# Attention and a gated MLP in one kernel: the first q and k loads uncast over hardware queues, cast on chip, with new instruction orders

## The chip, the cores and the metric

The kernel runs on one core of a Trainium2 chip. The metric is device time in microseconds (us). A run of a kernel is one execution, and the time before is the median of three such runs. The profile is one further execution, recorded instruction by instruction.

The engines are called by their short names: PE (TensorE, the matrix engine), ACT (ScalarE), DVE (VectorE), POOL (GpSimd) and SP (SyncE, which only issues transfers here). In the trace `PEld` is the load of a matrix operand, and `SPq`, `ACTq` and `POOLq` are issues of transfers from an engine's queue.

## The reference

Eight batches of eight heads, 576 tokens, head size 64, with 16 extra "beacon" keys and values ahead of each head's own. Causal attention, then an MLP with a sigmoid gate.

```python
B, H, S, Nb, D = (8, 8, 576, 16, 64)
k_all = concatenate([beacon_k, k], axis=2); v_all = concatenate([beacon_v, v], axis=2)
scores = matmul(q, k_all.transpose(0, 1, 3, 2)) / sqrt(D)
scores = where(causal, -1e9, scores)        # beacons are never masked
a = softmax(scores)
x = matmul(a, v_all)                        # -> (B * S, H * D) = (4608, 512)
h = x @ w_in                                # 512 -> 2048
g = h * (1 / (1 + exp(-1.702 * h)))
out = g @ w_out                             # 2048 -> 512, float32
```

All inputs and the output are float32 in HBM. On chip the matrix operands are 16 bit.

## The kernel before

**Attention.** Four heads make a *set*; a batch has two sets (`HS = 2`) and there are 16 in all. A set's q and k lie in `qn` and `kn` as 128 partitions (4 heads by 32) of token rows, are turned by DVE (`e_turn`, L422 and L429) into `qT` and `kT`, and give scores in the PSUM tile `s` (`e_qk`, L458). There is one such tile, four banks large, so the scores of a chunk can only start when ACT's exp (`e_exp`, L469) has read the chunk before. The exps go to `E`; masks are applied there by DVE or POOL (`e_mask`, L483 and L490). The value products (`e_av`, L546) take v from `vb`; the same function with ones gives the sums of the softmax, which DVE turns and inverts (`e_z1` L558, `e_z2` L565 and L569) and multiplies in (`e_norm`, L581) on the way to `xT`.

**The first two sets** are worked in halves. `ENDS = ((0, S), (0, HF), (HF, S))` with `HF = 256` names the whole set and its first and second part. `load_qk(s, which, part=1)` loads the first 256 tokens and `part=2` the other 320, so that chunks `qk0` and `qk1` (the first halves of sets 0 and 1) need only the first parts; `qk2` to `qk4` are the rest of set 0 and `qk5` to `qk7` the rest of set 1.

**MLP.** Tokens are taken in groups. `m1` products (`e_m1`) of groups 0 and 1 (256 tokens each) are gated by ACT's tanh (L628) and DVE (L647), later groups (512 tokens) by ACT's gelu (L635). The second product of groups 2 to 9 is made from seven products of quarter matrices (`products`), with sums by DVE in `sA` and `tB` (L679), and joins by DVE into `osb` (L744); the first two groups use `e_m2`. All of these go through `mm`: it issues one full-width matmul (L598) or, inside short pieces of work that lie between column-tiled value products, four of 32 columns (L601). Results are stored from SP (L676, L751).

**Loads.** q, k, v and both weight matrices are loaded by POOL (`nc.gpsimd.dma_start` at L368, L376 to L387, L393, L400), which casts float32 to 16 bit during the transfer. The beacon keys (`bkf`, L406) are loaded uncast by SP and ACT and cast by DVE (L412). `pool_load` keeps eight POOL transfers in flight: a ninth depends on the end of the one eight before.

**The order.** The function lists every piece of work as an `op` of a `Plan`, with an engine, a duration, and what it depends on. Tables written out by hand or by a search beforehand (`ORDER`) give the order of the ops on each engine. `Plan.run` walks these orders with the durations, gives each op a start, and sorts all ops by start; the instructions are then emitted in that sequence. The durations decide how the engines' emissions interleave and which PSUM tile a product gets, and the order on each engine is that of the table. One exception matters here: an op is emitted on whatever engine its function calls, at the place that its op has in the sequence.

**Fill.** Ahead of `qk0` and `qk1`, PE gets float32 matmuls on a scratch area whose results nobody reads (`FILL`, L1137). The scratch lies in `sA[0]`.

```python
FILL = {"qk0": (512, 384), "qk1": (256,)}
```

Of the kernel before, what the change touches and what calls it, by code (L numbers as in the profile page):

```python
# [8 lines left out]
F32 = mybir.dt.float32  # L9
# [8 lines left out]
        80, 106, 114, 123, 126, 144, 147, 116, 119, 159, 156, 135, 165, 128, 137, 162, 140, 168, 171, 231, 131, 133,  # L18
        149, 152, 154, 236, 174, 201, 238, 177, 192, 241, 195, 198, 204, 260, 180, 186, 207, 265, 187, 181, 188,
        267, 216, 210, 189, 270, 182, 213, 217, 401, 218, 183, 219, 404, 245, 250, 248, 279, 253, 407, 274, 255,  # L20
        284, 277, 282, 414, 222, 223, 224, 312, 292, 310, 225, 296, 308, 302, 290, 306, 320, 298, 294, 300, 314,
        304, 318, 316, 435, 426, 343, 365, 344, 423, 338, 339, 340, 341, 438, 345, 346, 349, 350, 429, 464, 351,
        433, 431, 366, 574, 359, 360, 352, 354, 355, 577, 361, 356, 474, 362, 357, 477, 583, 372, 373, 367, 368,
        480, 605, 482, 374, 484, 375, 607, 510, 490, 500, 496, 610, 492, 508, 506, 504, 498, 502, 488, 494, 486,
        514, 512, 596, 516, 534, 539, 540, 535, 593, 536, 545, 541, 537, 555, 742, 546, 601, 542, 556, 547, 745,
        622, 603, 557, 548, 619, 561, 748, 599, 550, 551, 562, 563, 755, 552, 564, 553, 629, 558, 776, 568, 627,
        625, 569, 570, 779, 635, 571, 651, 647, 655, 643, 631, 649, 633, 767, 805, 764, 653, 641, 774, 637, 639,
        657, 645, 818, 661, 659, 770, 679, 815, 684, 685, 772, 680, 686, 915, 681, 821, 690, 682, 687, 825, 918,
        706, 691, 823, 692, 713, 924, 693, 714, 700, 707, 715, 946, 708, 701, 695, 696, 697, 948, 702, 716, 698,
        703, 709, 951, 833, 851, 839, 827, 1083, 853, 831, 835, 855, 829, 934, 857, 937, 841, 837, 843, 849, 960,  # L30
        847, 845, 963, 875, 876, 940, 944, 877, 880, 881, 882, 886, 1086, 942, 878, 887, 883, 888, 1089, 891, 889,
        968, 892, 902, 1096, 893, 966, 903, 970, 904, 1117, 905, 894, 896, 909, 910, 1120, 897, 911, 898, 899, 912,
        1146, 984, 996, 988, 1256, 990, 1105, 992, 994, 998, 1002, 1000, 1108, 982, 972, 974, 1159, 976, 980, 1156,
        978, 986, 1111, 1041, 1020, 1042, 1113, 1043, 1115, 1021, 1022, 1259, 1031, 1023, 1025, 1026, 1032, 1027,
        1033, 1265, 1034, 1028, 1047, 1044, 1048, 1287, 1036, 1037, 1162, 1038, 1039, 1049, 1289, 1054, 1278, 1055,
        1050, 1056, 1275, 1057, 1292, 1166, 1180, 1164, 1178, 1172, 1182, 1186, 1198, 1304, 1188, 1281, 1301, 1285,
        1170, 1192, 1194, 1174, 1190, 1283, 1184, 1168, 1307, 1176, 1221, 1196, 1222, 1216, 1311, 1217, 1223, 1224,
        1309, 1218, 1227, 1219, 1228, 1229, 1230, 1243, 1244, 1245, 1232, 1237, 1233, 1234, 1317, 1238, 1235, 1239,
        1246, 1250, 1240, 1319, 1251, 1252, 1315, 1327, 1313, 1253, 1339, 1331, 1323, 1329, 1321, 1343, 1361, 1377,
        1341, 1362, 1337, 1325, 1335, 1333, 1363, 1366, 1367, 1364, 1368, 1372, 1369, 1373, 1374, 1375, 1382, 1383,  # L40
        1388, 1378, 1384, 1379, 1389, 1395, 1396, 1397, 1380, 1385, 1390, 1391, 1419, 1429, 1401, 1398, 1411, 1407,
        1423, 1403, 1421, 1405, 1409, 1431, 1425, 1413, 1417, 1415, 1449, 1450, 1460, 1427, 1451, 1454, 1455, 1470,
        1471, 1452, 1456, 1461, 1472, 1457, 1473, 1465, 1462, 1466, 1463, 1467, 1468, 1476, 1477, 1483, 1478, 1479,
        1484, 1485, 1486,
    ],
    "ACT": [
        3, 1, 83, 85, 109, 111, 115, 117, 120, 157, 136, 160, 138, 163, 166, 141, 169, 232, 172, 237, 175, 239, 178,
        193, 242, 196, 199, 202, 261, 205, 266, 208, 268, 190, 271, 211, 214, 402, 184, 220, 405, 408, 417, 415,
        313, 293, 226, 309, 311, 297, 307, 291, 321, 303, 295, 315, 301, 305, 299, 319, 317, 436, 342, 439, 468,
        465, 575, 578, 584, 587, 606, 608, 511, 501, 491, 493, 509, 497, 499, 505, 507, 495, 489, 503, 487, 513,  # L50
        515, 517, 611, 538, 743, 746, 749, 758, 756, 777, 780, 636, 652, 648, 656, 632, 644, 650, 634, 806, 642,
        638, 654, 658, 646, 640, 662, 660, 809, 916, 683, 919, 928, 925, 947, 949, 952, 834, 840, 854, 828, 852,
        832, 836, 856, 842, 858, 830, 844, 850, 838, 848, 846, 1084, 1087, 879, 1090, 1097, 1099, 1118, 1121, 1150,
        1147, 997, 989, 991, 985, 995, 993, 1003, 983, 999, 1001, 975, 973, 977, 979, 981, 987, 1257, 1260, 1024,
        1266, 1269, 1288, 1290, 1293, 1181, 1179, 1183, 1173, 1199, 1187, 1189, 1171, 1195, 1175, 1193, 1185, 1169,
        1191, 1177, 1197, 1220, 1318, 1320, 1328, 1314, 1316, 1332, 1324, 1340, 1322, 1344, 1330, 1342, 1338, 1326,
        1336, 1334, 1365, 1420, 1430, 1408, 1412, 1404, 1422, 1424, 1402, 1406, 1426, 1410, 1414, 1432, 1416, 1418,
        1428, 1453,
    ],
    "DVE": [  # L60
        77, 103, 78, 79, 104, 105, 88, 81, 86, 82, 87, 84, 113, 110, 112, 124, 125, 145, 98, 146, 127, 148, 93, 108,
        107, 158, 228, 129, 229, 257, 130, 161, 230, 164, 167, 170, 132, 134, 150, 151, 155, 153, 259, 173, 398,
        258, 176, 179, 194, 197, 200, 203, 209, 206, 399, 400, 215, 212, 411, 412, 413, 246, 247, 251, 252, 280,
        249, 254, 256, 275, 276, 281, 283, 278, 285, 286, 419, 420, 287, 463, 288, 289, 421, 461, 580, 330, 331,
        332, 422, 462, 322, 333, 323, 326, 327, 427, 324, 428, 334, 335, 424, 328, 336, 325, 337, 329, 425, 347,
        470, 430, 434, 581, 432, 471, 353, 472, 473, 582, 475, 478, 476, 479, 358, 363, 481, 369, 739, 483, 485,
        376, 752, 370, 741, 589, 740, 590, 754, 591, 615, 592, 526, 527, 753, 597, 598, 518, 519, 522, 523, 594,
        524, 520, 525, 595, 616, 530, 617, 618, 543, 602, 521, 531, 623, 604, 549, 620, 532, 528, 621, 529, 600,
        533, 624, 804, 554, 630, 559, 760, 626, 628, 565, 802, 566, 761, 572, 803, 921, 762, 811, 763, 812, 768,
        769, 765, 766, 775, 922, 813, 814, 663, 671, 672, 673, 819, 667, 674, 668, 771, 816, 664, 820, 665, 773,  # L70
        817, 666, 669, 822, 923, 1093, 675, 1080, 688, 676, 826, 670, 677, 824, 694, 678, 1081, 930, 699, 704, 710,
        717, 711, 1082, 931, 932, 956, 957, 1095, 933, 935, 938, 936, 958, 959, 939, 859, 1094, 961, 860, 964, 871,
        867, 863, 945, 872, 861, 868, 941, 864, 865, 866, 965, 873, 943, 869, 862, 1143, 962, 884, 870, 890, 874,
        1101, 969, 1102, 971, 967, 1144, 895, 1103, 1145, 906, 900, 913, 907, 1262, 1152, 1104, 1263, 1153, 1106,
        1154, 1109, 1110, 1107, 1155, 1157, 1160, 1012, 1016, 1013, 1014, 1112, 1004, 1008, 1017, 1005, 1009, 1114,
        1015, 1264, 1116, 1010, 1161, 1018, 1006, 1011, 1271, 1158, 1029, 1007, 1272, 1035, 1019, 1273, 1274, 1040,
        1163, 1045, 1279, 1051, 1276, 1058, 1052, 1297, 1167, 1298, 1299, 1280, 1300, 1165, 1277, 1305, 1282, 1302,
        1306, 1286, 1284, 1303, 1208, 1200, 1201, 1204, 1209, 1205, 1312, 1212, 1213, 1308, 1202, 1214, 1203, 1210,
        1211, 1310, 1215, 1206, 1225, 1207, 1231, 1236, 1241, 1247, 1248, 1254, 1345, 1346, 1347, 1348, 1357, 1349,
        1350, 1351, 1358, 1353, 1354, 1359, 1360, 1352, 1355, 1370, 1356, 1376, 1381, 1386, 1392, 1393, 1399, 1433,  # L80
        1434, 1435, 1436, 1437, 1438, 1439, 1441, 1440, 1442, 1445, 1446, 1447, 1448, 1443, 1458, 1444, 1464, 1469,
        1474, 1480, 1481, 1487,
    ],
    "POOL": [
# [22 lines left out]
}  # L107


class Op:  # L110
    __slots__ = (
        "eng", "dur", "deps", "pr", "due", "emit", "kind", "ring", "mode", "lat",
        "start", "end", "left", "users", "ready", "seq", "name", "count", "table",
    )


class Plan:


# [92 lines left out]
def kernel(  # L212
# [20 lines left out]
    Q = 4  # L233
# [935 lines left out]
```

## Time and profile before

| | before |
|---|---|
| time, median of 3 runs | 338.59 us (337.24 to 339.23) |
| profiled execution: time, span | 338.63 us, 336.9 us |
| PE busy | 313.6 us, 93% of the span |
| ACT, DVE, POOL busy | 200.8, 237.2, 119.6 us |
| moved by DMA queues | 29.09 MB, of them 18.50 MB by POOL's casting loads |
| score chunk `qk0` starts | 10.88 us |
| score chunk `qk2` starts | 18.29 us |
| first `m1` product starts | 24.10 us |

The span is what the trace covers; the time also has what lies around it, 1.7 us. In the page's second part the span is cut into 40 equal slices (8.4 us each), and each digit is the busy share of one slice in tenths. Busy times of different engines overlap. `PEclk` is the granted clock of PE. A line of the chain of waits has a start, a length, and the engine and line, or the transfer, that was being waited for. A line of the list of transfers has the issuing queue, the count, the size as written on chip, and the median time from issue to landing.

### The profile page before, as it was taken

How to read it: one execution, taken by the hardware profiler on the slowest of the kernel's cores; microseconds unless marked ns; L12 is line 12 of the kernel's file. 1: busy time of each engine (PE TensorE's matmuls, PEld its weight loads, DVE VectorE, ACT ScalarE, POOL GpSimd, SP SyncE). 2: the span in 40 equal slices, each digit the busy share in tenths (PEclk: the TensorE clock that was granted, in tenths of full speed). 3: DMA queues.
4: the chain of work that ended last, by engine and by line, in shares of the span. 5: the costliest groups of instructions: out<-in, count | busy, mean ns of one | idle time of the engine just before them, and what ended most of it. 6: DMA issues, size and time to landing. Idle time of an engine off the chain costs nothing.

```text
span 336.9 us, 13766 instructions
## 1 busy us (share of the span) xinstructions
PE 313.6 (93%) x6274; PEld 221.4 (66%) x6274; DVE 237.2 (70%) x479; ACT 200.8 (60%) x236; POOL 119.6 (36%) x182
## 2 busy tenths in 40 slices
PE   3369999999989998999999899999999999999995
PEld 1256775654768466845888888657875786586484
DVE  2485944879988879997977879866986464163164
ACT  1347787765957786679767576768665503622620
POOL 7847458394131806182048204540611000000000
PEclk9998999999999999999999999999999999999999
DMA  4999999799251974696149603650230001002003
GB/s 47 171 168 181 205 172 161 153 97 189 20 101 38 159 48 66 121 133 95 28 60 157 108 6 71 110 43 5 21 101 30 4 33 62 33 31 90 6 22 105
DMA packets 61819, 29.09 MB, mean 86 GB/s; under 512 B 44352, under 2 KB 57664, under 8 KB 61760
## 3 DMA queue, kind: packets, MB, share of 16 engines
q0 software_dynamic: 51200, 18.50, 48.9%
q1 hardware_dynamic: 10464, 9.69, 8.7%
q8 instruction: 49, 0.80, 1.0%
q14 instruction: 10, 0.08, 0.1%
q10 hardware_dynamic: 96, 0.02, 0.0%
HBM read 37.22 MB, written 9.44 MB: 139 GB/s over the span
## 4 chain that ended last, share of the span: by engine, by line
PE 78%; DVE 8%; DMA 6%; ACT 4%; issue 3%; POOL 0%; DVEq 0%; ACTq 0%; POOLq 0%
PE u L598 40%; PE u L601 22%; PE u L546 8%; PE s L458 8%; DMA kn<-in_k_dram 4%; ACT E L469 3%; DMA qn<-in_q_dram 2%; DVE sA L679 1%; DVE osb L744 1%; ACT g L635 1%; DVE zs L508 1%; DVE zt L558 1%; ACT L635 1%; DVE kT L429 1%; DVE rz L569 1%
## 5 line engine op out<-in xcount | busy, mean ns | idle before, releaser
L469 ACT ACTIVATE E<-s 128x2048 f16<-128x2048 f32 (+4 forms) x66 | 98.9, 1515 | 55.6 <-PE s L458 54.1
L635 ACT ACTIVATE g<-u 128x512 f16<-128x512 f32 x128 | 69.7, 598 | 55.0 <-PE u L598 38.4
L490 POOL TENSOR_SCALAR_AFFINE_SELECT E<-E 128x512 f16<-128x512 f16 (+3 forms) x78 | 52.2, 686 | 106.4 <-ACT E L469 104.8
L598 PE MATMUL u<-xT,w 128*128 128x512 f16 (+1 forms) x456 | 87.2, 346 | 0.0
L598 PEld LDWEIGHTS <-w 128*128 128x128 f16 x456 | 44.1, 99 | 35.1 <-DVE osb L744 0.2
L744 DVE SCALAR_TENSOR_TENSOR osb<-u,osb 128x512 f32<-128x512 f32 x56 | 37.4, 683 | 24.2 <-PE u L598 21.1
L601 PE MATMUL u<-xT,w 128*32 128x512 f16 (+1 forms) x992 | 47.0, 338 | 1.1 <-issue 0.9
L458 PE MATMUL s<-qT,kT 32*128 32x32 f16 (+17 forms) x1376 | 35.6, 233 | 13.3 <-DVE kT L422 5.9
L458 PEld LDWEIGHTS <-kT 32*128 32x128 f16 x1376 | 26.0, 95 | 31.0 <-issue 19.4
L598 PE MATMUL u<-w,g 128*128 128x256 f16 (+1 forms) x232 | 37.9, 302 | 0.0
L598 PEld LDWEIGHTS <-g 128*128 128x128 f16 x324 | 30.9, 98 | 10.3
L601 PEld LDWEIGHTS <-w 128*32 128x32 f16 x992 | 27.1, 96 | 14.1 <-issue 1.9
L546 PE MATMUL u<-E,vb 128*32 128x352 f16 (+9 forms) x928 | 31.1, 266 | 1.0 <-DVE osb L744 0.4
L387 POOL DMA_DIRECT2D vb<-in_v_dram x32 | 27.5, 859 | 11.7 <-PE u L546 11.1
L581 DVE TENSOR_TENSOR xT<-u,rz 128x352 f16<-128x352 f32 (+3 forms) x48 | 25.5, 546 | 7.2 <-PE u L546 6.9
L601 PE MATMUL u<-w,g 128*32 128x256 f16 x864 | 29.7, 273 | 0.0
L546 PEld LDWEIGHTS <-vb 128*32 128x32 f16 (+1 forms) x928 | 23.7, 98 | 6.4 <-issue 1.7
L508 DVE TENSOR_TENSOR zs<-zs,E 128x1344 f16<-128x1344 f16 (+2 forms) x36 | 23.5, 654 | 5.1 <-POOL E L490 4.4
L679 DVE TENSOR_TENSOR sA<-g 128x512 f16<-128x512 f16 x32 | 13.2, 426 | 19.7 <-ACT g L635 19.6
L601 PEld LDWEIGHTS <-g 128*32 128x32 f16 x1008 | 25.9, 97 | 1.7 <-issue 0.3
L429 DVE STREAM_TRANSPOSE kT<-kn 128x576 f32<-128x576 f32 (+2 forms) x18 | 20.4, 1131 | 9.0 <-DMA kn<-in_k_dram 8.5
L598 PEld LDWEIGHTS <-sA 128*128 128x128 f16 x224 | 21.5, 98 | 3.5
(52 smaller groups left out, 335.1 us busy)
## 6 DMA issues: line engine op xcount, KB each, us to landing
out_dram<-osb SPq DMA_DIRECT2D x36, 256.0 KB, 2.8
kn<-in_k_dram POOLq DMA_DIRECT2D x14, 288.0 KB, 5.7
qn<-in_q_dram POOLq DMA_DIRECT2D x14, 288.0 KB, 5.6
vb<-in_v_dram POOLq DMA_DIRECT2D x24, 128.0 KB, 4.3
w<-in_moe_w_in_dram POOLq DMA_DIRECT2D x8, 256.0 KB, 8.4
w<-in_moe_w_out_dram POOLq DMA_DIRECT2D x4, 512.0 KB, 10.0
vb<-in_v_dram POOLq DMA_DIRECT2D x8, 112.0 KB, 5.1
vb<-in_v_dram POOLq DMA_DIRECT2D x8, 80.0 KB, 4.5
```

Source lines behind the costliest of these rows:

```text
L387: nc.gpsimd.dma_start(out=t[0 : hi - lo, j, h0:h1, :], in_=v[b, h0:h1, lo:hi, :].rearrange("h n d -> n h d"),)
L429: nc.vector.transpose(out=f32(dst.rearrange("p n e -> p (n e)")).rearrange("p (r t) -> p t r", t=n), in_=f32(src[:, a // 32 * D : e // 32 ...
L458: nc.tensor.matmul(sc[:, h, o : o + w], kT[s % NB2][r : r + 32, j * P : (j + 1) * P, d], qT[s % NB2][r : r + 32, a : a + w, d], start=(d = ...
L469: nc.scalar.activation(out=Es[s][:, :, c0:c1], in_=ss[i][:, :, o : o + c1 - c0], func=AFT.Exp, scale=0.125,)
L490: nc.gpsimd.affine_select(out=blk, in_=blk, compare_op=ALU.is_ge, fill=0.0, base=off + (Nb if j == 0 else 0), pattern=[[0, Q], [1, w]], ch ...
L508: nc.vector.tensor_tensor(out=t, in0=E[:, :, Z0:S] if i == 1 else t, in1=E[:, :, wcol[i] : wcol[i] + S - a], op=ALU.add,)
L546: nc.tensor.matmul(u[32 * h : 32 * h + 32, a:e], lhs, src[0:kw, h, col : col + e - a], start=first, stop=last,)
L581: nc.vector.tensor_tensor(out=xT[:, 2 * hs + x : 2 * hs + x + n, t0 : t0 + w], in0=rings[("av", s, x, half)][:, 0 : n * w].rearrange("p (n ...
L598: nc.tensor.matmul(o, lhs, rhs, start=start, stop=stop)
L601: nc.tensor.matmul(o[r : r + 32], lhs[:, r : r + 32], rhs, start=start, stop=stop)
L635: nc.scalar.activation(out=gts[g][:, n0:n1, 0:w], in_=rings[("m1", g, n0)][:, 0 : n * w].rearrange("p (n w) -> p n w", n=n), func=AFT.Gelu ...
L744: nc.vector.scalar_tensor_tensor(out=osbs[(g, dst)][:, :], in0=rings[("p", g, p)][:, :], scalar=scale_of(g), in1=osbs[(g, src)][:, :], op0 ...
```

## The change

**First halves and second halves of the first two sets.** The eight loads by POOL with a cast go. Instead `e_fetch` copies float32 into staging areas (`staged`) that lie in the tiles `sA` and `tB`, which nothing else uses so early, and `e_cast` casts from there into `qn` and `kn`: ACT casts the four first parts (512 columns), POOL the four second parts (640 columns).

```diff
+    def staged(s, which, part):
+        i = 2 * s + which
+        n = (ENDS[part][1] - ENDS[part][0]) // 32 * D
+        t = (sA[1], sA[2], sA[1], sA[2])[i] if part == 1 else (tB[0], tB[1], tB[2], sA[0])[i]
+        x = 4 * (i // 2) if part == 1 else 0
+        return t[:, x : x + n // (HM // 2), :].rearrange("p a n -> p (a n)").bitcast(F32)
+
+    def e_fetch(s, which, part, e):
+        b, hs = divmod(s, HS)
+        a, z = ENDS[part]
+        (nc.sync if e == "SP" else nc.scalar).dma_start(
+            out=staged(s, which, part),
+            in_=(q, k)[which][b, Q * hs : Q * hs + Q, a:z].rearrange("h (r t) d -> h r (t d)", r=32),
+        )
+
+    def e_cast(s, which, part, e):
+        a, z = ENDS[part]
+        dst = (qn, kn)[which][s % NB3][:, a // 32 * D : z // 32 * D]
+        (nc.scalar.copy if e == "ACT" else nc.gpsimd.tensor_copy)(out=dst, in_=staged(s, which, part))
...
+    def fetch_qk(s, which, part, e):
+        a, z = ENDS[part]
+        x = op(e, 450, [], lambda: e_fetch(s, which, part, e), name=f"hk{s}.{part}")
+        x = op("Q", 1560 * (z - a) / S, [x], lambda: None, name=f"hk{s}.{part}q")
+        e = ("", "ACT", "POOL")[part]
+        ld_qk[(s, which, part > 1)] = op(
+            e, 65 + 0.8345 * 2 * (z - a) if e == "ACT" else 140 + 0.95 * 2 * (z - a), [x],
+            lambda: e_cast(s, which, part, e), name=f"cast{s}.{part}",
+        )
...
-    load_bk(0, HS, (), ("SP", "ACT"))
     for s in range(HS):
-        load_qk(s, 1, part=1)
-        load_qk(s, 0, part=1)
+        fetch_qk(s, 1, 1, "SP")
+        fetch_qk(s, 0, 1, "ACT")
+        if s == 0:
+            load_bk(0, HS, (), ("SP", "ACT"))
...
     for s in range(HS):
-        load_qk(s, 1, part=2)
-        load_qk(s, 0, part=2)
+        for which in (1, 0):
+            fetch_qk(s, which, 2, "SP")
```

**Which queue they are on.** In `fetch_qk` the name `e` is given a new value before the first lambda is called. In the plan and in `ORDER` six of the eight loads are ops of SP and two of ACT. In the program that is built all eight are on ACT's queue, in this order:

```
ACT: load q0 first, load q1 first, beacons, beacons, load k0 first, load k0 second, table load,
     cast q0, load k1 first, cast q1, load q1 second, load q0 second, cast k0, load k1 second, cast k1, exps ...
POOL: v, v, keep masks, v, beacon v, cast k0 second, cast q0 second, w1 x5, q of set 2, cast k1 second, w1,
      k of set 2, w1, cast q1 second, mask, w1, v ...
```

**Orders.** All tables of `ORDER` are new. On PE, the value products of set 0's first half now stand ahead of `qk2`:

```
before: qk0 qk1 qk2 av0.2.0 av0.0.0 av1.2.0 av1.0.0 qk3 qk4 m1.0.2 m1.0.0 qk5
after:  qk0 qk1 av0.2.0 av0.0.0 qk2 av1.2.0 av1.0.0 qk3 qk4 m1.0.0 m1.0.2 qk5
```

The second products of group 0 start earlier in the order (after `qk10` instead of after `qk12`). Of the products that `mm` issues, 596 are issued as four of 32 columns, and before 660; PE's rows go from 12,541 to 12,156.

**Scratch, fill and plan.** The scratch moves to `tB[0]`, and the fill of `qk0` is smaller. Some durations in the plan are new, and the rule of eight POOL transfers in flight moves from dependencies into `Plan.run`.

```diff
-    scrap = sA[0][:, 0:4, :].rearrange("p a n -> p (a n)").bitcast(F32)
+    scrap = tB[0][:, 5:8, :].rearrange("p a n -> p (a n)").bitcast(F32)
...
-    FILL = {"qk0": (512, 384), "qk1": (256,)}
+    FILL = {"qk0": (384, 384), "qk1": (256,)}
...
+                    if o.lands is not None and len(flight) >= self.LANES:
+                        if flight[-self.LANES].end is None:
+                            break
+                        t = max(t, flight[-self.LANES].end + self.LAT["Q"])
...
-            return 300 if d.eng == "SP" else 1200
+            return 1200 if d.eng == "POOL" else 300
+        if d.name.startswith("hk"):
+            return 800
...
-                    d = 50 + 4 * (e - a) / 1.92 if eng == "DVE" else 140 + 0.875 * 4 * (e - a)
+                    d = 50 + 4 * (e - a) / 1.92 if eng == "DVE" else 190 + 0.9 * 4 * (e - a)
...
-            prev = [op("DVE", 1550, w2_ld + (prev if i < 3 else [tds[0]]), lambda i=i: e_t(i, "DVE"), pr=3, due=TDUE, name="t")]
+            prev = [op("DVE", 1200, w2_ld + (prev if i < 3 else [tds[0]]), lambda i=i: e_t(i, "DVE"), pr=3, due=TDUE, name="t")]
```

## The prediction

> **What bounds the kernel now.** I read the page first, for which engine is full and when.
>
> ```profile
> span 336.9 us, 13766 instructions
> PE 313.6 (93%) x6274; PEld 221.4 (66%) x6274; DVE 237.2 (70%) x479; ACT 200.8 (60%) x236; POOL 119.6 (36%) x182
> PE   3369999999989998999999899999999999999995
> PEclk9998999999999999999999999999999999999999
> DMA  4999999799251974696149603650230001002003
> ```
>
> TensorE is busy 93%, so the rest of the kernel is its work in a row; only 336.9 - 313.6 = 23.3 us are idle. The digits put most of that in the first three slices (8.4 us each). The stretches of the windows view (engine busy, clock, DMA share) give sizes:
>
> ```profile
> 0.00:25.00 25.00, 11.32 (x213) 7.54 (x214) 12.04 (x35) 8.38 (x8) 16.97 (x30) 0.99 1.11 128
> 25.00:320.00 295.00, 289.52 (x5952) 203.03 (x5951) 215.95 (x426) 190.40 (x226) 102.63 (x153) 0.99 0.57 84
> 320.00:336.90 16.90, 12.79 (x114) 10.84 (x111) 9.22 (x19) 2.02 (x4) 0.00 (x0) 0.95 0.19 64
> ```
>
> Idle: 13.7 us before 25, 5.5 in the 295 us of the body, 4.1 at the end. The start is the only large hole. The chain of waits says what fills it (start, length, what):
>
> ```profile
> 2.15 6.97 DMA kn<-in_k_dram
> 9.41 7.96 DMA qn<-in_q_dram
> 17.39 0.74 DVE qT L429
> 18.29 0.88 PE s L458 x18
> ```
>
> Two transfers, 15 us in all: first k, then the second half of set 0's q. The timeline fits: qk0 starts at 10.88, qk1 at 13.52, then TensorE stands until qk2 at 18.29, and the first input product m1.0 starts at 24.10. The list of DMA issues shows what a queue costs:
>
> ```profile
> kn<-in_k_dram POOLq DMA_DIRECT2D x2, 128.0 KB, 6.3
> qn<-in_q_dram POOLq DMA_DIRECT2D x2, 160.0 KB, 8.7
> out_dram<-osb SPq DMA_DIRECT2D x36, 256.0 KB, 2.8
> bkf<-in_beacon_k_dram ACTq DMA_DIRECT2D x2, 8.0 KB, 1.8
> ```
>
> Last column: us to landing. GpSimd's casting loads take 6.3 to 8.7, plain transfers from SP and ACT 1.8 to 2.8.
>
> [...] clock 0.69 in 25 to 30 us and 0.96 in 20 to 25 make 3.5 us at half rate, in which m1.0's first 16 matmuls took 3.11 us where sixteen later ones took 1.92. [...]
>
> **The change part by part.**
>
> *Where the loads are issued.* The source says SP for six of the eight and ACT for two. The lambda reads `e` when it is called, and by then `e` is ACT or POOL, so in the built order all eight stand on ACT's queue, between its casts, and SP gets none. ACT issues in order: q0, q1, two beacon loads, k0, second half of k0, table load, cast q0, k1, cast q1, second halves of q1 and q0, cast k0, second half of k1, cast k1, then the exps. I cost that order, not the intended one.
>
> *Prices.* One ACT issue: 0.45 (two took 0.89); SP's 128-partition stores took 0.37; I take 0.4. Landing of 256 KB: 2.6, from 1.8 (the beacon load) to 6.1 (the slowest of all stores). A 512-column ACT cast: 0.6 (mean of the 128x512 ACT rows, 0.595[...]). GpSimd's cast of 640 columns: 0.9, from its 512-column mask of 0.73[...].
>
> *qk0.* ACT starts at 0.8 (the barrier): six issues to 3.2, table load 1.28 to 4.5, cast q0 to 5.1 (landed at 3.4), k1 issued to 5.5, cast q1 to 6.1, two issues to 6.9, cast k0 to 7.5 (landed at 5.0). VectorE's turn of k, 0.64 and 0.2 of signalling: 8.4. qk0 at 8.6, against 10.88: -2.3.
>
> *qk1, qk2.* qk0 0.9, exps 1.6: qk1 at 11.3 (13.52 before; one score tile, so it waits for the exps). Its exps end at 13.95. Set 0's second q half, issued by 6.9, lands at 9.5; GpSimd casts to 10.4; VectorE turns by 11.4. Landing at 6.1 it would be 14.9, 0.8 later. So the last to arrive at qk2 is now exp 1, and qk2 starts near 14.1, against 18.29: **-4.2**. That is the DMA stall gone; what is late next is the chain score, exp, score.
>
> *To m1.0.* exp 2 to 16.6, qk3 16.9 (two value products stand before it, 1.4 us, behind masks ending at 15.2), exp 3 to 19.1, qk4 to 19.8. m1.0 needs set 0 and 1's normalised halves: value products done 16.7, then VectorE's z1, two z2 (0.65 each), two norms (0.66 each), ready at 19.1. m1.0 at 19.8, against 24.10: **-4.3**. It also needs two w1 loads; they stand on POOL behind both casts of set 0, so go out from 10.4 to 11.8 and, with the median 8.4 us to landing, arrive by 20.2: level, 0.4 late at worst. Six more w1 loads (1.5 MB at the 165 to 200 GB/s of that stretch: 8 to 9 us) land before 30; their last users come after qk8 and qk9. Before, the two first w1 loads were issued at 6.28, so this cover is thinner than it was.
>
> *The clock.* [...] Gone, the window at 24.6 to 28 saves up to 1.7 us; another may fall on the new m1.0 instead. I take 0, -1.7 to +1.2.
>
> *The body's new orders.* Matmuls and columns are the same; 596 products run as four 32-column pieces instead of 660. A piece costs no more: 32 of them, eight products, take 0.87 us in the chain, 0.109 a product, as plain ones of 256 columns step. Changes between full, row-tiled and column-tiled work go from 110 to 112. One costs about 0.085 us (m1 at 41.16 to 43.51 holds 1.75 of product, 0.43 of score steps and two changes): +0.2. TensorE's rows fall to 12,156[...]; its waits put to issue sum to 2.5 us, so at most -2.5, taken as 0. What the reordering does to the 5.5 us of idle body the trace cannot show: -5.5 if all go, +5 if they double; taken as 0. ACT's table loads stay 14. The end keeps prod 3 last; the joins after it move by under 0.2.
>
> *The rest at nothing.* GpSimd's four casts (3.6 us) lie before its first mask at 18.6, on an engine busy 36%; the planner's new durations and lane rule issue nothing; the scratch for the fill matmuls moves and shrinks (0.85 instead of 1.14 a piece), before 8.6. If that cover goes, w1 is late, and that is the last rival.
>
> **Sum:** the profiled execution of before took 338.63 (span 336.9 and 1.7 around it), level with the median of 338.59. 338.63 - 4.3 + 0.2 = **334.5**.
>
> **The rivals.**
> - *Main, 0.66:* as above, 331.8 to 336.6: clock and body take or give 2, slow landings 0.8 (landing at 4.6: qk0 at 9.5, m1.0 3.5 earlier).
> - *More, 0.10:* the half-rate window goes and half the body's idle too: 334.5 - 1.7 - 2.7 = 330.1. For it: every idle us of the body is one of order. Against: new idle comes as easily.
> - *The start gains, the body gives it back, 0.14:* [...] an order laid for loads on SP meets loads on ACT. If the body's idle goes from 5.5 to 9.5: 338.5. Against: once TensorE is full (from 28 us on before) a start moved by 1 us shifts everything alike.
> - *GpSimd held at its cast, 0.10, slower:* POOL waits for set 0's second q half with all of w1 behind it. Landing L after 6.9: the second w1 load arrives at 6.9 + L + 0.9 + 1.4 + 8.4 = 17.6 + L. Free to L = 2.2; as before (24.1) at 6.5; slower by 0.5% from about 8.2. L = 10, near the slowest k load of the first 20 us (10.5), gives 27.6: 338.6 + 3.5 = 342.1. For it: GpSimd's loads show such landings. Against: theirs only; plain stores took at most 6.1, beacon loads 6.6.
> - *It doesn't do what it says* is taken up in the first part: without SP the ACT queue serialises; issued on SP, k0 would come some 2 us sooner, which exp 1 then bounds anyway.
>
> **How the numbers follow.** 0.5%, 1.7 us, is about what a measurement of this kernel can tell from no change: faster is under 336.9, slower over 340.3. Faster 0.66 + 0.10 + 0.03 of the third case = 0.79; same 0.11; slower 0.10. The range runs from 331.0 (leaves out about half of "more") to 338.4 (leaves out the last case and some of the third).
>
> **What would show it.** Right: q and k's halves land within 2 to 5 us from ACT's queue; qk0 near 8.6, qk2 near 14, straight after exp 1, m1.0 near 20; TensorE's first 25 us about 4 us less idle; body idle 4 to 7 us. Wrong: a wait of w on DMA ahead of m1.0, POOL standing at its casts past 12 us, body idle of 9 us and more, or m1.0 later than 22.

## The result, and the profile after

The changed kernel takes **354.81 us** (median of 6 runs, 353.06 to 357.44) against 339.23 for the kernel before (6 runs, 337.24 to 341.09). The ratio is 1.0462 (1.0407 to 1.0517). The forecast was 334.5. The profiled execution took 354.64 us with a span of 352.9, which is 16.0 us more than before.

From the page of the changed kernel:

```profile
span 352.9 us, 13390 instructions
...
PE 315.8 (89%) x6082; PEld 221.7 (63%) x6082; DVE 237.8 (67%) x479; ACT 203.9 (58%) x240; POOL 120.3 (34%) x178
...
PE   3114899999999999999999989999999999999995
...
DMA  7326999998958271379407991047041004102002
...
q10 hardware_dynamic: 1152, 2.38, 2.0%
```

TensorE is as busy as before (315.8 us, before 313.6), so the added time is idle time. The digits 1, 1 and 4 in the second to fourth slice (8.8 to 35 us) hold it. In the same slices the digits of the DMA engines are *low*: 3, 2 and 6, where the kernel before had 9s. Transfers are late while the DMA engines have room: they are 0.30 busy from 8 to 20 us. The last line is the queue that carries q and k: 1152 packets, 2.38 MB.

The same stretches as before, and one more, in the windows view (columns: us, then busy time of PE, PEld, DVE, ACT, POOL, then clock, DMA share, GB/s):

```profile
0.00:25.00 25.00, 5.75 (x54) 3.14 (x54) 4.95 (x15) 5.27 (x7) 5.11 (x13) 1.00 0.46 87
25.00:320.00 295.00, 281.19 (x5840) 199.03 (x5832) 219.86 (x437) 189.14 (x216) 115.19 (x165) 1.00 0.60 89
```
```profile
8.00:20.00 12.00, 2.04 (x26) 1.17 (x26) 2.39 (x7) 1.57 (x3) 0.72 (x1) 1.00 0.30 83
```

The DMA share is the number of packets under way divided by 16, so it can pass 1 (from 8 to 20 us it was 1.45 in the kernel before). Here it is 0.30, at 83 GB/s. Counted in the packets of the trace, the median number of q and k packets under way at once is 4.

TensorE's timeline has the starts that the prediction's path to m1.0 runs over:

```profile
16.40 0.89 PE L488 MATMUL s<-qT,kT 32*128 32x256 f16 x24 [11.94 <-DVE bkn L442]
...
24.22 0.90 PE L488 MATMUL s<-qT,kT 32*128 32x256 f16 x24 [5.77 <-ACT E L499]
30.73 0.66 PE L576 MATMUL u<-E,ones 128*32 128x256 f16 x12 [5.62 <-DVE E L513]
...
32.05 0.88 PE L488 MATMUL s<-qT,kT 32*128 32x320 f16 x24
```
```profile
37.96 3.59 PE L628 MATMUL u<-xT,w 128*128 128x256 f16 x16
```

qk0 starts at 16.40 (forecast 8.6), qk1 at 24.22 (11.3), qk2 at 32.05 (14.1), m1.0 at 37.96 (19.8). The chain of waits of this execution reaches back over its last quarter only. So the start is read from ACT's timeline, with the issues of its queue (`ACTq`) in it:

```profile
0.80 1.69 ACTq L393 DMA_DIRECT2D sA<-in_q_dram  x2
...
3.52 0.62 ACTq L393 DMA_DIRECT2D sA<-in_k_dram  x1
...
7.72 0.62 ACT L401 CAST qn<-sA 128x512 f16<-128x512 f32 x1 [1.61 <-DMA sA<-in_q_dram]
...
11.13 0.62 ACT L401 CAST qn<-sA 128x512 f16<-128x512 f32 x1 [2.80 <-DMA sA<-in_q_dram]
11.14 3.88 ACTq L393 DMA_DIRECT2D tB<-in_q_dram  x2
15.06 0.62 ACT L401 CAST kn<-sA 128x512 f16<-128x512 f32 x1 [3.31 <-DMA sA<-in_k_dram]
15.08 3.12 ACTq L393 DMA_DIRECT2D sA<-in_k_dram  x1
22.03 0.62 ACT L401 CAST kn<-sA 128x512 f16<-128x512 f32 x1 [6.36 <-DMA sA<-in_k_dram]
```

Every cast waits for its transfer. Counted from issue to cast, q0 takes some 6.9 us (0.80 to 7.72), k0 11.5 us (3.52 to 15.06), k1 14.3 us (7.72 to 22.03). In the packets of the queue the eight loads end at about 6.6, 10.5, 14.4, 18.3, 21.7, 25.3, 28.4 and 31.6: one every 3.1 to 3.9 us, one after another as if through a narrow pipe. POOL has the same wait, in its timeline:

```profile
18.71 0.72 POOL L401 CAST kn<-tB 128x640 f16<-128x640 f32 x1 [13.02 <-DMA tB<-in_k_dram]
28.91 0.72 POOL L401 CAST qn<-tB 128x640 f16<-128x640 f32 x1 [9.48 <-DMA tB<-in_q_dram]
29.57 2.81 POOL L423 DMA_DIRECT2D w<-in_moe_w_in_dram  x4
```

POOL stands 22.5 us at two casts. VectorE then stands at the turn of set 0's second q half (29.66) with the masks behind it. PE's value products wait for those masks (30.73), and qk2 stands behind the value products.

**Why so narrow.** The load's source is `"h (r t) d -> h r (t d)"`, and its slowest dimension is the four heads. The same number is in the packets: 4 under way, and, besides 32 packets of the two beacon loads, 32 packets of 4 bytes on the queue at the ends of the loads, four for each. The author's estimate from this is that the slowest dimension sets how many packets of a load can be under way, and that all eight loads share the same 4. The trace does not name the DMA engine of a packet, so how a load is divided among them was not shown. The runs below test the estimate.

### The profile page after: what moved, and what is told of

It is laid out like the page before. It is cut to its first block, busy times and chain, and to the rows that moved or that the text cites. A ratio compares the mean times of both kernels' runs of the same rounds, so it can differ in the third digit from the quotient of the medians.

```text
span 352.9 us, 13390 instructions
## 1 busy us (share of the span) xinstructions
PE 315.8 (89%) x6082; PEld 221.7 (63%) x6082; DVE 237.8 (67%) x479; ACT 203.9 (58%) x240; POOL 120.3 (34%) x178
## 3 DMA queue, kind: packets, MB, share of 16 engines
q10 hardware_dynamic: 1152, 2.38, 2.0%
## 5 line engine op out<-in xcount | busy, mean ns | idle before, releaser
L499 ACT ACTIVATE E<-s 128x2048 f16<-128x2048 f32 (+5 forms) x66 | 99.0, 1516 | 51.7 <-PE s L488 50.2
L520 POOL TENSOR_SCALAR_AFFINE_SELECT E<-E 128x512 f16<-128x512 f16 (+2 forms) x78 | 55.6, 733 | 101.2 <-ACT E L499 94.6
L628 PE MATMUL u<-xT,w 128*128 128x512 f16 (+1 forms) x476 | 88.5, 342 | 0.0
L628 PEld LDWEIGHTS <-w 128*128 128x128 f16 x476 | 46.3, 100 | 35.4 <-DMA w<-in_moe_w_in_dram 0.3
L774 DVE SCALAR_TENSOR_TENSOR osb<-u,osb 128x512 f32<-128x512 f32 x56 | 37.3, 681 | 18.3 <-PE u L628 15.2
L628 PE MATMUL u<-w,g 128*128 128x256 f16 (+1 forms) x288 | 45.8, 297 | 0.4 <-DVE g L709 0.4
L628 PEld LDWEIGHTS <-g 128*128 128x128 f16 x380 | 35.7, 98 | 11.5 <-DVE g L709 0.6
L631 PEld LDWEIGHTS <-w 128*32 128x32 f16 x912 | 25.2, 96 | 14.2 <-issue 1.0
L459 DVE STREAM_TRANSPOSE qT<-qn 128x576 f32<-128x576 f32 (+2 forms) x18 | 20.2, 1125 | 19.2 <-ACT qn L401 8.8
L576 PE MATMUL u<-E,vb 128*32 128x208 f16 (+9 forms) x928 | 30.3, 266 | 1.6 <-DVE osb L774 1.5
L631 PE MATMUL u<-w,g 128*32 128x256 f16 x640 | 21.9, 273 | 0.3 <-issue 0.2
```

Of the source, the lines that this page charges most:

```text
L459: nc.vector.transpose(out=f32(dst.rearrange("p n e -> p (n e)")).rearrange("p (r t) -> p t r", t=n), in_=f32(src[:, a // 32 * D : e // 32 ...
L499: nc.scalar.activation(out=Es[s][:, :, c0:c1], in_=ss[i][:, :, o : o + c1 - c0], func=AFT.Exp, scale=0.125,)
L520: nc.gpsimd.affine_select(out=blk, in_=blk, compare_op=ALU.is_ge, fill=0.0, base=off + (Nb if j == 0 else 0), pattern=[[0, Q], [1, w]], ch ...
L576: nc.tensor.matmul(u[32 * h : 32 * h + 32, a:e], lhs, src[0:kw, h, col : col + e - a], start=first, stop=last,)
L628: nc.tensor.matmul(o, lhs, rhs, start=start, stop=stop)
L631: nc.tensor.matmul(o[r : r + 32], lhs[:, r : r + 32], rhs, start=start, stop=stop)
```

## The experiments

The theory, A in the expectations of `sp_queue`, `pairs`, `heads_sp` and `old_whole`, is this one: the slowest dimension sets how many packets are under way. Its rivals are the wrong queue (all eight issues on ACT, blocked behind casts), the new orders, and the uncast route itself. Runs that were made together share their runs of the kernel before.

**The queue: `sp_queue`.** The lambda gets its own `e`, so that six loads go out from SP.

```diff
-        x = op(e, 450, [], lambda: e_fetch(s, which, part, e), ...)
+        x = op(e, 450, [], lambda e=e: e_fetch(s, which, part, e), ...)
```

> The changed kernel with one edit: the lambda keeps the queue that the plan names, so six of the eight loads go out on SP and two on ACT. Theory A ([...] all eight together are 2.36 MB at some 88 GB/s, 27 us): nearly nothing, the last needed load still lands near 27 us, first m1 product near 36 instead of 38, time 351 to 355. Theory B (ACT's queue is what is slow, its issues standing behind casts that wait): the loads land within 6 us of issue, m1 starts near 20 to 24, time 336 to 342.

Measured: 354.17 us (2 runs) against 339.54 (43 runs), ratio 1.0417 (1.0344 to 1.0490). m1.0 starts at 37.57. The windows view:

```profile
8.00:20.00 12.00, 2.05 (x26) 1.19 (x26) 2.39 (x7) 1.85 (x3) 0.72 (x1) 1.00 0.30 87
```

Two queues instead of one, and the same share of 0.30 at 87 GB/s. From 8 to 12 us both queues have loads under way, a median of 2 packets each, and together still 4, as many as one queue has in the changed kernel. The time is in the range of theory A; the queue is not the cause.

**Slowest dimension 2: `pairs`.** Each load of the changed kernel is cut in two loads of two heads, on the same queue. Same bytes, same packets.

```diff
+        for h in range(0, Q, 2):
...
-            out=staged(s, which, part),
-            in_=(q, k)[which][b, Q * hs : Q * hs + Q, a:z].rearrange(...),
+                out=staged(s, which, part)[32 * h : 32 * (h + 2)],
+                in_=(q, k)[which][b, Q * hs + h : Q * hs + h + 2, a:z].rearrange(...),
```

> The changed kernel with each of the eight loads cut in two loads of two heads each, same bytes, same queue. Theory A [...]: [...] the 2.36 MB take some 54 us instead of 27, transfers run at about 45 GB/s with about 2 packets in flight, first m1 product at 60 to 68, time 377 to 388. Theory B (the cost lies in the queue, per issue): eight more issues of 0.55 us on ACT, time near 359. Theory C (contention with POOL's loads of v): unchanged, 353 to 357.

Measured: 376.08 us (1 run), m1.0 at 58.34.

```profile
8.00:20.00 12.00, 0.00 (x0) 0.00 (x0) 0.64 (x1) 1.90 (x2) 0.00 (x0) 1.00 0.16 42
```

About half the share (0.16) and half the rate (42 GB/s), with a median of 2 packets under way, and two packets of 4 bytes for each load. The time is just under theory A's 377 to 388. A division that leaves every byte and the size of every data packet as they were more than doubles the time added: some 36 us instead of 15.

**Slowest dimension 32: `heads_sp` and `heads`.** Each load is cut in four, one head each. The head's dimension has size 1, so the slowest is now the 32 of `r`. In `heads_sp` the lambda is mended as well; in `heads` all 32 issues stay on ACT.

```diff
+        for h in range(0, Q, 1):
...
+                out=staged(s, which, part)[32 * h : 32 * (h + 1)],
+                in_=(q, k)[which][b, Q * hs + h : Q * hs + h + 1, a:z].rearrange(...),
```

> The changed kernel with the loads on SP and ACT as the plan has them, and each load cut in four, one head each, so that the slowest dimension is the 32 row groups. Theory A [...]: 8 times 4 issues of 0.3 to 0.5 us, loads land within 3 us, qk0 near 10, qk2 near 15, first m1 product near 21 instead of 38, time 336 to 340 (the body of the new orders being some 2 us longer than before's). Theory B (queue, per issue): 32 issues cost more than 8, time 355 or more.

> The changed kernel with each load cut by head, [...] but all 32 issues on ACT's queue, where the changed kernel has them. [...] By hand: 16 issues of 0.45 to 0.55 us before set 0's last half is out, between waiting casts: qk0 near 18 to 20, set 0's second q half landing near 21, first m1 product 28 to 32, time 345 to 350. If the queue is no cost even then: as with SP and ACT, 342 to 344.

Measured: `heads_sp` 342.88 us (20 runs) against 339.54, ratio 1.0093 (1.0072 to 1.0115), m1.0 at 25.76. `heads` 344.91 us (1 run) against 340.31, m1.0 at 27.67, a little less than its 345 to 350 and 28 to 32. `heads_sp`:

```profile
8.00:20.00 12.00, 3.80 (x75) 2.70 (x79) 5.44 (x16) 6.69 (x9) 3.40 (x5) 1.00 0.58 144
```

The share goes from 0.30 to 0.58 and the rate from 87 to 144 GB/s, though four times as many issues of some 0.4 us each must go out. 354.17 - 342.88 = **11.3 us** come back by the cut alone. In both kernels the 32 loads end with 16 packets of 4 bytes each, and up to 17 packets of q and k are under way at once (median 8 from 2 to 18 us). Over the three kernels the rate per packet under way stays alike: 42 / (0.16 x 16), 87 / (0.30 x 16) and 144 / (0.58 x 16) are 16, 18 and 16 GB/s. It is the number of packets under way that changes.

`heads_sp` missed theory A's 336 to 340 us all the same, and its start is at 25.76 instead of near 21. The eight issues of the second q halves stand on SP from 11.93 to 15.60, and GpSimd's cast of set 0's half waits for it until 17.32: here the issues take the time. With the loads cut by head the queue does count: one queue against two is 1.4 to 2 us (344.91, a single run, against 342.88; by ratios to their own runs of the kernel before, 1.0135 against 1.0093).

**The orders alone: `orders_only`.** The changed kernel with casting loads by POOL in place of the uncast loads, at the same places of the plan, and without the casts.

```diff
-        (nc.sync if e == "SP" else nc.scalar).dma_start(
-            out=staged(s, which, part),
+        nc.gpsimd.dma_start(
+            out=(qn, kn)[which][s % NB3][:, a // 32 * D : z // 32 * D],
```

> The changed kernel's orders and plan, but the eight loads are casting loads by POOL again, issued at the place of the plan's loads, and the casts on ACT and POOL are gone. What is left of the change is the new orders. If they cost what the traces' difference after the first m1 product says (310.9 us to the last matmul instead of 308.7): start as before within 1.5 us, time 339.5 to 342.5. If the orders are as good as the old ones: 337 to 339.5. If the late start itself made the body longer: also 337 to 339.5.

Measured: 340.89 us (22 runs) against 339.54, ratio 1.0039 (1.0021 to 1.0057): **+1.3 us**. qk0 starts at 11.94 and m1.0 at 24.92; before, 10.88 and 24.10. The new orders load and turn both q ahead of the first k, so k is turned at 11.24 where before both were done by 10.84. The rest of the 1.3 us, behind m1.0, is not placed: single executions differ by more than that.

**Whole sets: `old_pool_whole`, `old_whole`, `new_whole`, `new_pool_whole`.** If the shape of a transfer matters this much, the halves may be the wrong shape in the kernel before too. Here sets 0 and 1 come whole: once by POOL's casting loads, once uncast with `(h r)` as one dimension of 128 (k on SP, q on ACT, staged in `xT`, cast by DVE and ACT). Each is tried in the orders of before (`old`) and of after (`new`). The shape in the two uncast ones:

```diff
-            in_=(q, k)[which][b, Q * hs : Q * hs + Q, a:z].rearrange("h (r t) d -> h r (t d)", r=32),
+                in_=(q, k)[which][b, Q * hs : Q * hs + Q].rearrange("h (r t) d -> (h r) (t d)", r=32),
```

and in `old_pool_whole`:

```diff
-            out=dst[:, a // 32 * D : e // 32 * D],
-            in_=(q, k)[which][b, Q * hs : Q * hs + Q, a:e].rearrange("h (r t) d -> h r (t d)", r=32),
+                out=dst[:, :],
+                in_=(q, k)[which][b, Q * hs : Q * hs + Q].rearrange("h (r t) d -> h r (t d)", r=32),
```

> The kernel before, its orders and plan unchanged, with sets 0 and 1 loaded whole: four uncast loads (k on SP, q on ACT) whose source is 128 contiguous rows of 4.6 KB, staged in xT; ACT casts q, VectorE casts k, and each is turned in one piece of 576 columns; the second loads and turns are gone. Theory A [...]: each load lands within 3 to 5 us of issue at 15 or so packets in flight, qk0 near 9, qk2 straight after exp 1 near 14, first m1 product near 20 against 24.1, time 333.5 to 336.5. Theory B (uncast loads from hardware queues are slow beside GpSimd's, whatever their shape; twice the bytes on chip): qk0 later than 12, time 339 or more.

> The kernel before with sets 0 and 1 loaded whole by GpSimd's casting loads, as the later sets are, and turned in one piece; no staging, no casts. It has the wide shape without the hardware queues. If the shape alone gives the gain: loads land 5 to 6 us after issue, qk0 near 10, m1 near 20.5, time 334 to 337. If the queue gives it: as before or slower, since set 0 now waits for 2.25 times the bytes: qk0 near 12 to 13, m1 near 23, time 337.5 to 341.

> The changed kernel's orders with the four whole loads of old_whole (k on SP cast by VectorE, q on ACT cast by ACT). Start as in old_whole, m1 near 20 to 21, and the new orders' 1.3 us (measured without the loads) on top: 335 to 338. If the new orders are right for an early start and were only starved: as old_whole or faster.

> The changed kernel's orders, sets 0 and 1 loaded whole by casting loads of GpSimd at the places where the plan has the uncast loads; no staging, no casts. Theory A (loads and orders add up): the new orders cost 1.3 us with halves cast in flight (340.9 against 339.5), so 338.0 + 1.3 = 339.3, range 338.5 to 340.3, m1.0 at 21.5 to 23.5. Theory B (the orders cost only where they meet the halves): as new_whole, 336.5 to 338.2.

| q, k of sets 0 and 1 | orders before | orders after |
|---|---|---|
| halves, cast by POOL's loads | 1 (before) | 340.89, 1.0039 (1.0021 to 1.0057) |
| halves, uncast | not run | 354.81, 1.0462 (1.0407 to 1.0517) |
| whole, cast by POOL's loads | 338.01, 0.9927 (0.9898 to 0.9955) | 338.64, 0.9961 (0.9941 to 0.9981) |
| whole, uncast, 128 rows | 341.38, 1.0048 (1.0024 to 1.0071) | **337.27, 0.9910** (0.9883 to 0.9937) |

Three of the four whole-set kernels are faster than the kernel before by their intervals, though by less than 1%; `new_whole` (4 runs) has the best ratio, though its interval overlaps that of `old_pool_whole` (7 runs). That one lies between its two expectations: qk0 at 10.35 as for a gain by shape, m1.0 at 22.09 and 338.01 us short of it. With POOL's whole loads the new orders cost 0.0034, or 1.2 us, about what they did with halves; the two intervals overlap, but the value is near what adding up gave for `new_pool_whole`.

The list of DMA issues in the first 12 us shows what whole loads do. Before:

```profile
kn<-in_k_dram POOLq DMA_DIRECT2D x2, 128.0 KB, 6.3
qn<-in_q_dram POOLq DMA_DIRECT2D x2, 128.0 KB, 7.4
```

`old_pool_whole`:

```profile
kn<-in_k_dram POOLq DMA_DIRECT2D x2, 288.0 KB, 4.7
qn<-in_q_dram POOLq DMA_DIRECT2D x2, 288.0 KB, 7.0
```

`new_whole`:

```profile
xT<-in_q_dram ACTq DMA_DIRECT2D x2, 576.0 KB, 4.6
xT<-in_k_dram SPq DMA_DIRECT2D x2, 576.0 KB, 7.6
```

More than twice the data in less time for POOL's loads, and for q; only k in `new_whole` takes longer (7.6 against 6.3). The queues of `new_whole` carried 16 packets of 4 bytes for each whole load. In those 12 us POOL's queue moved 0.91 MB in 3782 packets before and 1.59 MB in 1917 packets with whole loads: 240 bytes a packet against 830, weights and v included.

`old_whole` missed the 333.5 to 336.5 us that a pure gain at the start would have given. In the old order set 1's k goes first on SP: it was issued at 1.54 and landed at 5.74, while set 0's k, issued at 2.47, landed only at 10.88, and set 0's q was turned behind it. qk0 started at 14.21. In `new_whole` set 0's k goes first, was issued at 1.99 and landed at 8.98, with q already turned, and qk0 started at 11.46. Besides, POOL's weight loads go out from 2.83 in the old order and from 5.67 in the new one, and move their bytes beside q and k. How much of the difference each of these makes has not been tried; DVE casts k in both.

**What then holds the start: `old_pool_fill`, `new_whole_fill`.** In `old_pool_whole` and `new_whole` m1.0's first 16 matmuls take 3.6 us, against 1.92 in `orders_only`, and a score chunk 0.88 instead of 0.57. More filling matmuls ahead of qk0 were to tell whether TensorE's idle time causes that.

```diff
-    FILL = {"qk0": (512, 384), "qk1": (256,)}
+    FILL = {"qk0": (512, 512, 512, 512, 384), "qk1": (256,)}
```

(in `new_whole_fill` six pieces of 384 instead of two)

> The kernel before with sets 0 and 1 loaded whole by GpSimd (338.0 us, 0.9927 of before), plus 2432 instead of 896 columns of filling matmuls ahead of qk0, which there starts at 10.35 after 5.3 us of idle TensorE. Theory A: the half rate at the start (QK chunks of 0.88, m1.0's 16 matmuls in 3.59 us at 22) is a matter of TensorE's earlier activity: filled without a gap, qk0's chunk takes about 0.57, the 16 matmuls 1.9, and the kernel 335.5 to 336.7, 0.986 to 0.989 of before. Theory B: the rate rises at some 25 us whatever was done: 16 matmuls in 3.4 to 3.6, 337.5 to 339, or up to 1 us more if the fill runs past qk0's inputs.

> The changed kernel's orders with the four whole uncast loads (337.3 us, 0.991 of before), plus 2304 instead of 768 columns of filling matmuls ahead of qk0, which there starts at 11.46 after 7.0 us of idle TensorE. Theory A (the half rate follows from idle time): QK chunks 0.57, m1.0's 16 matmuls 1.9, start of m1.0 21.5 to 22.6, 334.3 to 336, 0.983 to 0.987 of before. Theory B (it rises at 25 us whatever was done): 16 matmuls in 3.4 to 3.6, 336.8 to 338.3.

Measured: `old_pool_fill` 337.21 us, 0.9929 (0.9904 to 0.9954); `new_whole_fill` 337.85 us, 0.9945 (0.9905 to 0.9985); the kernel before 340.06. In time, no difference from the same kernels without the longer fill that these runs can tell. TensorE's timeline of `old_pool_fill`:

```profile
9.86 0.57 PE L461 MATMUL s<-qT,kT 32*128 32x256 f16 x24 [1.72 <-DVE kT L425]
...
12.26 0.57 PE L461 MATMUL s<-qT,kT 32*128 32x256 f16 x24 [1.20 <-DVE qT L432]
14.58 0.88 PE L461 MATMUL s<-qT,kT 32*128 32x320 f16 x24 [1.75 <-ACT E L472]
...
21.04 2.88 PE L601 MATMUL u<-xT,w 128*128 128x256 f16 x16
```

The fill does bring full rate to qk0 and qk1 (0.57), and it is lost again by qk2 (0.88), after a start with gaps of 1.2 and 1.75 us before qk1 and qk2. In `new_whole_fill` only qk0 ran at full rate (0.57); qk1 took 0.90 and the 16 matmuls 3.59. Theory A is right on the first chunks and wrong on the gain. What would keep the rate up to m1.0 stays open.

## Why the prediction was wrong

**The step that failed** is the price "Landing of 256 KB: 2.6, from 1.8 to 6.1". It was taken from transfers of other shapes: stores of the same size from 128 partitions, and the small beacon loads. It was also given to each load as if it were alone, though four or five are under way at a time. Measured, up to the cast: 6.9 us for the first load, then 11.5 and 14.3, with a median of 4 packets of all the loads under way: an estimate from the traced rate, 2.36 MB at 83 to 87 GB/s, gives 27 to 28 us for all eight, and the last ended at 31.6. That moves the start: set 0's second q half was ready for its cast at 28.91 instead of 9.5. (Counted from 6.9, L is 22.0, of which 8.1 pass before its issue ends at 15.02.) The formula of the rival, 17.6 + L, gives m1.0 at 39.6, measured 37.96. That it comes so near is in part luck: it runs through w1, but the second w1 load had landed at 36.56, and m1.0 came behind set 0's score chunks, 5.9 us after qk2.

By its other steps:

- *All eight loads on ACT's queue, in that order:* right. "An issue 0.4": mostly too low, 0.85 each for the first two and 0.6 for k's, and under backlog 3.88 for the two at 11.14 and 3.12 for the one at 15.08. It does not matter here: `sp_queue` takes six of the eight issues off ACT and gains 0.6 us, within the scatter.
- *Casts:* 0.62 on ACT (forecast 0.6): right. 0.72 on POOL (0.9): a fifth less.
- *Last to arrive at qk2 is exp 1:* wrong, for the same reason. It is the second q half, by way of POOL's cast, DVE's turn and the masks behind it. From qk2 on the chain is as drawn: m1.0 follows 5.9 us later, forecast 5.7.
- *w1 level with m1.0:* right in so far as m1.0 did not wait for it. The w1 loads went out from 29.57 instead of 10.4, the first two landed at 33.99 and 36.56, and m1.0 started at 37.96, since all else was later still.
- *The clock, 0 (-1.7 to +1.2):* m1.0's 16 matmuls took 3.59 us, before 3.11: +0.5, within the range. The picture behind it was incomplete. The kernel before has no clock record until 21.23, and its score chunks took 0.88 to 0.90 us up to 18.29 and 0.56 at 21.34: it ran at half rate there too, not only in the window from 24.64, where the record shows a clock of 0.50 for 3.41 us. In the changed kernel the half rate lasted until 43.27.
- *The new orders, +0.2:* mis-sized. `orders_only` gives +1.3 (0.7 to 1.9), part of it from the order of q and k, which the prediction did not price.

With measured terms the added time splits into +13.9 for the start (m1.0 at 37.96 against 24.10) and +2.1 for everything from m1.0 to the end of the span (314.9 against 312.8): 338.63 + 13.9 + 2.1 = 354.6. By experiments, of the 15.6 us: the orders 1.3; uncast loads, casts and 32 issues 2.0 (340.89 to 342.88); loads with a slowest dimension of 4 instead of 32 11.3 (342.88 to 354.17). The rest is 1.0: 0.6 between `sp_queue` and the changed kernel, and 0.3 between the two sets of runs of the kernel before. Both are within the scatter of the runs.

**The rivals.** The one that ended slower, "GpSimd held at its cast", had the right wait: POOL stood past 12 us and m1.0 came later than 22, both named as signs of being wrong. It was priced at L = 10 at most and given one chance in ten, and it had w1 as the victim; the victim was q itself, and L was 22. The evidence against it, "plain stores took at most 6.1", was the same error of shape.

## What to carry to other kernels

Price a load by the dimensions of its access pattern before its bytes: here a source whose slowest dimension is 4 had a median of 4 packets under way, and eight such loads ended one behind the other, 3.1 to 3.9 us apart. If many transfers are late while the DMA share is low, look at the shape: the share from 8 to 20 us was 0.30 with that source, and 0.58 with a slowest dimension of 32. Loading whole sets, with `(h r)` merged into 128 rows, k on SP and the casts on ACT and DVE, turned a loss of 4.6% into a gain of 0.9% over the kernel before. Whole casting loads by POOL in the old orders gave a gain of 0.7%, so the route of the loads itself showed no gain that can be told apart.

## What the runs showed of the hardware

- An issue on ACT's queue is not free when transfers back up: 3.12 us for one load (15.08), against 0.5 to 0.85 for those up to 7.72. It stands in line with ACT's casts: k0's load had ended at about 14.4, and its cast started at 15.06, behind the two issues that ended at 15.02. On SP in `sp_queue` the last load's issue took as long (14.94 to 18.04).
- TensorE worked at about half rate where the clock column reads 1.00: m1.0's 16 matmuls took 3.59 us at 37.96 in the changed kernel, and 1.92 at 24.92 in `orders_only`, with 1.00 in both. The clock records of these traces begin only at 43.27 and at 22.38, and where there is no record the column shows 1.00. The score chunks are at half rate ahead of the first record, and from it on they follow the records: in the changed kernel 0.88 at 34.60 and 0.56 at 44.40 (both 24 matmuls of 224 columns), in `orders_only` 0.88 at 19.48 and 0.56 at 26.78 (both 24 of 320); in the kernel before, with records from 21.23, 0.88 at 18.29, 0.56 at 21.34, and again 0.88 at 27.14, where the record is 0.50. Read the rate there from durations of equal matmuls, not from the column.
- The shape of a load from ACT or SP shows in its packets: those of 4 bytes that end it were 2, 4, 16 and 16 for loads whose slowest dimension was 2, 4, 32 and 128, and the median number of data packets under way was 2, 4, 8 and 15 (`pairs`, the changed kernel, `heads_sp`, `new_whole`).
- POOL's casting loads, too, moved more in the same time when they came whole: 288 KB in 4.7 to 7.0 us against 128 KB in 6.3 to 7.4.
